# A tuned attention and feed-forward kernel: the last four key heads gathered by small DMAs, value products in pairs, another layer norm write and start-up order

## The chip, the cores and the metric

The kernel runs on one core of a Trainium2 chip. The metric is the device time of one execution in microseconds (us). The span in a profile is a little shorter (165.6 us for an execution of 167.3 us). In the profiles PE is TensorE, the matrix engine (PEld: its weight loads), DVE is VectorE, ACT is ScalarE, POOL is GpSimd and SP is SyncE, which issues most DMAs (data transfers) of this kernel from one queue, one after the other. The issue time of a DMA is how long its queue is occupied with starting it. PSUM banks hold PE's products until DVE or ACT has copied them. A run is called slow when it is over 1.5% above the fastest run of the same kernel.

## The reference, cut to what matters

```python
def _A_ref(x, wqkv, wo):                      # attention: 16 heads of 28 features
    W, dil = 8, 2                             # 8 keys back, every second one
    qkv = (x @ wqkv) ...                      # split into q, k, v
    idx = pos[:, None] - off[None, :]         # off = 0, 2, ..., 14
    logits = einsum("bhsd,bhswd->bhsw", q, kg) * scale
    attn = softmax(where(mask, logits, -1e9))
    return einsum("bhsw,bhswd->bhsd", attn, vg) ... @ wo

def _B_ref(x, w1, b1, w2, b2):                # feed forward, 448 -> 1792 -> 448
    return gelu(x @ w1 + b1) @ w2 + b2

xn = layernorm(x)                             # x: 1 x 2048 x 448
return x + _A_ref(xn, wqkv, wo) * silu(_B_ref(xn, ...))
```

## The kernel before: the parts that the argument touches

The sequence is cut into four chunks of 512 positions and, for attention, into 17 units of 121 queries. While the second FFN product of one chunk runs, the attention units of that chunk are laid between. PE's work in program order for one chunk (`n = c + 1` is the chunk whose q, k and v are being made):

```python
for c in range(3):
    feed_forward_1(c, ps, ...)          # 14 tiles of w1, gelu, the first q/k pair of the next chunk,
                                        # wo jobs of the chunk before
    qk_pair(n, 1, True, DD)
    for i in range(5):                  # five attention units
        b = next(units)
        if i == 0:
            E = qk_unit(b, lambda: qk_pair(n, 2, False, ...))   # scores S, exp and mask on ACT and DVE
            ...
            qk_pair(n, 3, True, DA)     # the fourth q/k pair stands between S and psO
        else:
            E = qk_unit(b)
            norm()
            ffn2_job(4 * c + i - 1)     # ps_y
            v_job(next(vs))             # one value product a unit
            if n + 1 < NC:
                ln_apply(4 * n + 3 + i)
                ln_dma(4 * n + 3 + i)   # DMA transpose on SP, into xnT
        norm = av_unit(b, E)            # psO
    ...
    ps = ffn1(n, 0, True)
```

Loads and stores, all issued by SP, in order:

```python
def late_loads():                       # before: issued before the first chunk's FFN
    nc.sync.dma_start(b2bc[:], ...)
    nc.sync.dma_start(x_sb[3][:, :, :], dram_rows(x_par, 12, 4))
    for g in range(4):
        for h in range(4):              # 16 loads of 28 rows from DRAM
            r = (4 * g + h) * DH
            nc.sync.dma_start(wo[32 * h + 1:32 * h + 1 + DH, g, :], A_wo[r:r + DH, :])

def wo_put(t, ps, cs=slice(0, D)):
    sg = ...
    o_t = work.tile([P, D], BF16, name="o_t", tag="o_t", bufs=3)    # three output buffers
    nc.vector.tensor_tensor(out=o_t[:, cs], in0=xt(t)[:, cs], in1=sg[:, cs], op=ALU.add)
    nc.sync.dma_start(dram_rows(out_par, t, 1)[:, 0, cs], o_t[:, cs])
```

The softmax here doesn't subtract the row's maximum and nothing guards it: scores larger than these inputs give would overflow.

Of the kernel before, what the change touches and what calls it, by code (L numbers as in the profile page):

```python
# [8 lines left out]
F32 = mybir.dt.float32  # L9
# [19 lines left out]
EPS = 1e-5  # L29
NG = 12  # L30


@with_exitstack
def kernel(
# [37 lines left out]
    g_sb = [big.tile([P, D], BF16, name=f"g_{i}") for i in range(NG)]  # L72
    wraw = work.tile([P, KT, 2 * D + 8], BF16, name="wraw", tag="stage", bufs=1)
    wv = big.tile([P, KT, D], BF16, name="wv")
    wqk = big.tile([P, KT, 2 * H, 32], BF16, name="wqk")
    w1 = big.tile([P, KT, F], BF16, name="w1")
# [19 lines left out]

    nc.vector.memset(wraw[:, :, 2 * D:2 * D + 8].bitcast(U32), 0)
    nc.vector.memset(wz[:].bitcast(U32), 0)
# [7 lines left out]
    for w in range(2):  # L106
        nc.sync.dma_start(wraw[64 * w:64 * w + 64, 3, D * w:D * w + D], A_wqkv[384:448, D * w:D * w + D])
    nc.sync.dma_start(b1r[:], B_b1.rearrange("(m f) -> m f", f=P))
    nc.sync.dma_start(x_sb[1][:, :, :], dram_rows(x_par, 4, 4))
    for c0, c1 in ((0, F // 2), (F // 2, F)):  # L110
        nc.sync.dma_start(w1[:, 0:3, c0:c1], B_w1[0:384, c0:c1].rearrange("(k p) f -> p k f", p=P))
        for r in (0, 64):
            nc.sync.dma_start(w1[r:r + 64, 3, c0:c1], B_w1[384:448, c0:c1])
    nc.sync.dma_start(x_sb[2][:, :, :], dram_rows(x_par, 8, 4))
    nc.sync.dma_start(w2[:, :, :], B_w2.rearrange("(m p) c -> p m c", p=P))

# [10 lines left out]
    nc.vector.memset(wv[64:128, 3, :].bitcast(U32), 0)  # L127
    nc.vector.memset(wraw[0:64, 3, D:D + 8].bitcast(U32), 0)
    nc.vector.memset(wo[:, :, :].bitcast(U32), 0)
# [4 lines left out]
    def late_loads():  # L134
        nc.sync.dma_start(b2bc[:], B_b2.rearrange("(o d) -> o d", o=1).to_broadcast((P, D)))
        nc.sync.dma_start(x_sb[3][:, :, :], dram_rows(x_par, 12, 4))
        for g in range(4):
            for h in range(4):
                r = (4 * g + h) * DH
                nc.sync.dma_start(wo[32 * h + 1:32 * h + 1 + DH, g, :], A_wo[r:r + DH, :])  # L140
# [27 lines left out]
    def ln_apply(t):  # L168
        nc.vector.tensor_scalar(xnb[t % 4][:, 0:D], xt(t), mv[:, t, 0:1], rstd[:, t:t + 1],
                                op0=ALU.subtract, op1=ALU.mult)  # L170

        nc.vector.tensor_copy(xnb[t % 4][:, D:512], xnb[t % 4][:, D - 64:D])

# [12 lines left out]

    def qk_weights(which, kt):

        r = slice(0, P) if kt < 3 else slice(64 * which, 64 * which + 64)
        src = wraw[r, kt, D * which:D * which + 32]  # L190
        nc.vector.tensor_copy(wqk[r, kt, H * which:H * which + H, :],
                              bass.AP(src.tensor, src.offset, [list(src.ap[0]), [DH, H], [1, 32]]))

# [18 lines left out]

    def qk_put(c, g, w, ps, copies):
        copies[w]((qT, kT)[w][:, g, LEAD + c * CH:LEAD + (c + 1) * CH], ps[w][:, :])  # L214

    def qk_pair(c, g, even, copies):

        ps = [psB.tile([P, CH], F32, name="ps_qk", tag="B") for _ in range(2)]
        for f in ((qk_full, qk_rest), (qk_rest, qk_full))[not even]:
            f(c, g, ps, f is (qk_full, qk_rest)[not even], copies)  # L220

    DA, DD = (nc.vector.tensor_copy, nc.scalar.copy), (nc.vector.tensor_copy, nc.vector.tensor_copy)

    def v_mm(b):
        ps = psB.tile([P, D], F32, name="ps_v", tag="B")
        o = LEAD + QB * b - 7
        for kt in range(KT):
            nc.tensor.matmul(ps[:, :], xnT[:, kt, o:o + P], wv[:, kt, :],  # L228
                             start=(kt == 0), stop=(kt == KT - 1))
        return ps  # L230
# [4 lines left out]
    def v_job(b):  # L235
        v_put(b, v_mm(b))


# [37 lines left out]

    def ffn2_job(t, put=True):
        tt = t % 4
        ps = psB.tile([P, D], F32, name="ps_y", tag="B")
        for m in range(MT):  # L280
            nc.tensor.matmul(ps[:, :], hT[:, m, tt * P:(tt + 1) * P], w2[:, m, :],  # L281
                             start=(m == 0), stop=(m == MT - 1))
        if put:
            ffn2_put(t, ps)
        return ps

# [104 lines left out]
    def feed_forward_1(c, ps, wos):  # L391

        nc.scalar.preload_act_table_set(SET_GELU)
        gelu(0, ps)
        for k in range(1, MT // 2):
            if (c, k) in ((0, 6), (1, 4), (2, 4)):

                qk_pair(c + 1, 0, True, DD)
            odd = k in {0: (1, 3, 5, 6), 3: (1, 3, 5)}.get(c, (1, 3, 4, 6))
            ps = ffn1(c, k, not odd)  # L400
            gelu(k, ps)
            if c + 2 < NC and k in (1, 3):
                for t in range(4 * c + 7 + k, 4 * c + 9 + k):
                    ln_stats(t)
            if k in ((3, 5, 6) if c == 3 else (4,)):
                for _ in range(4 if c == 2 else 2):
                    if wos:
                        wo_job(wos.pop(0))
            if c and k in (3, 5):
                silu_job(4 * (c - 1) + k - 3)  # L410
                silu_job(4 * (c - 1) + k - 2)
        nc.scalar.preload_act_table_set(SET_EXP)


    with tc.manual_schedule(engines={ENG.PE, ENG.Activation, ENG.DVE, ENG.Pool, ENG.SP}):
        nc.scalar.preload_act_table_set(SET_EXP)
        busy(9)
        ln_stats(0)
# [14 lines left out]
        ln_rstd(3, 1)  # L433
        v_put(0, v0)
        ln_apply(2)
        pT.append(ln_tr(2))
        v1 = v_mm(1)
        ln_put(2, pT[2])
        v_put(1, v1)
        ln_apply(3)  # L440
        pT.append(ln_tr(3))
        v2 = v_mm(2)
        ln_put(3, pT[3])
        v_put(2, v2)
        v_job(3)
        pb = psB.tile([P, MT], BF16, name="pb", tag="B")
        nc.tensor.transpose(pb[:, :], b1r[:, :], ident[0:MT, 0:MT])
        for which in range(2):
            for kt in range(KT):
                qk_weights(which, kt)  # L450
        y_sb = work.tile([P, 4, D + 4], F32, name="y", tag="stage", bufs=1)
        late_constants()
# [9 lines left out]
        for t in range(4, 8):  # L462
            ln_apply(t)
            ln_dma(t)
        late_loads()

        units = iter(range(NB))
        for c in range(3):
            feed_forward_1(c, ps, [[], [0, 1], [2, 3, 4, 5]][c])
            n = c + 1  # L470
            qk_pair(n, 1, True, DD)
            norm = lambda: None
            vs = iter(range(4 * n, 4 * n + (5 if c == 2 else 4)))
            for i in range(5):
                b = next(units)
                if i == 0:
                    tail = []
                    E = qk_unit(b, lambda: qk_pair(n, 2, False, (nc.vector.tensor_copy, lambda *a: tail.append(a))))
                    if n + 1 < NC:
                        ln_rstd(4 * n + 4, 4)  # L480
                    nc.scalar.copy(*tail[0])
                    qk_pair(n, 3, True, DA)
                else:
                    E = qk_unit(b)
                    norm()
                    ffn2_job(4 * c + i - 1)
                    v_job(next(vs))
                    if n + 1 < NC:
                        ln_apply(4 * n + 3 + i)
                        ln_dma(4 * n + 3 + i)  # L490
                norm = av_unit(b, E)
            norm()
            for b in vs:
                v_job(b)
            ps = ffn1(n, 0, True)
        feed_forward_1(3, ps, [6, 7, 8, 9, 10, 11])
# [58 lines left out]
```

## Time and profile before

| | before |
|---|---|
| median of four runs | 167.72 us (167.32 to 167.9) |
| span in the profile | 165.6 us |
| PE busy | 158.9 us, 96% of the span |
| chain that ended last | 83% PE |
| granted clock of PE | 1.000 |

### The profile page before, as it was taken

Reading aid. Unit: us, or ns where it says so; the run is one execution under the profiler, and the core shown is the slowest. Engines: PE = TensorE matmul, PEld = TensorE weight load, DVE = VectorE, ACT = ScalarE, POOL = GpSimd, SP = SyncE. Lnnn points to the kernel's source line nnn. Section 1 sums busy time; section 2 is a strip of 40 time slices with the busy share of each in tenths; the row PEclk is TensorE's granted clock in tenths of the full one; section 3 lists DMA queues with packets and bytes.
Section 4 is the critical chain, followed back from the end, with each engine's and each line's share of the span. In section 5 each row is a group of like instructions: output and inputs, shape, how many; then the busy total and the mean of one; then the engine's idle time right before and its main releaser. Section 6 shows DMA issues by size and latency. Waiting matters only on the chain.

```text
span 165.6 us, 3242 instructions
## 1 busy us (share of the span) xinstructions
PE 158.9 (96%) x1290; PEld 71.8 (43%) x1301; DVE 112.9 (68%) x256; ACT 125.9 (76%) x198; POOL 4.5 (3%) x16
## 2 busy tenths in 40 slices
PE   6899999999999999999999999999999999999990
PEld 2343333345554334445554334335555334445570
DVE  5967890497888638687888308877777507678893
ACT  3773698598887795998887795698888698698830
POOL 7002000000000000000000000000000000000000
PEclk9999999999999999999999999999999999999999
DMA  5999995520111100100211100300000002020011
GB/s 134 302 306 267 325 190 93 164 44 4 32 36 32 32 0 4 55 0 0 36 32 32 36 0 0 112 1 4 0 4 0 0 0 60 31 83 0 4 55 55
DMA packets 15963, 10.62 MB, mean 64 GB/s; under 512 B 7500, under 2 KB 15948, under 8 KB 15948
## 3 DMA queue, kind: packets, MB, share of 16 engines
q1 hardware_dynamic: 15660, 10.18, 24.0%
q10 hardware_dynamic: 288, 0.23, 0.5%
q8 instruction: 10, 0.16, 0.4%
q14 instruction: 5, 0.04, 0.1%
HBM read 7.00 MB, written 1.84 MB: 53 GB/s over the span
## 4 chain that ended last, share of the span: by engine, by line
PE 83%; ACT 7%; DVE 5%; DMA 2%; issue 1%; DVEq 0%
PE ps_y L281 23%; PE ps_h L249 21%; PE ps_qk L197 11%; PE ps_v L228 8%; PE ps_s L331 6%; PE ps_h L258 4%; PE S L355 3%; PE psO L370 3%; ACT hT L264 3%; PE ps_qk L207 3%; DMA x<-in_A_x_dram 2%; ACT th L310 1%; DVE sg L337 1%; DVE st L161 1%; ACT L509 1%
## 5 line engine op out<-in xcount | busy, mean ns | idle before, releaser
L264 ACT ACTIVATE hT<-ps_h,b1f 128x512 bf16<-128x512 f32 x56 | 34.1, 695 | 10.1 <-PE ps_h L258 7.3
L249 PE MATMUL ps_h<-xnT,w 128*128 128x512 bf16 x161 | 39.3, 380 | 0.5 <-issue 0.2
L281 PE MATMUL ps_y<-w,hT 128*128 128x448 bf16 x196 | 39.5, 353 | 0.0
L361 ACT ACTIVATE E<-S 128x976 bf16<-128x976 f32 x34 | 31.6, 983 | 2.1 <-PE S L355 0.8
L281 PEld LDWEIGHTS <-hT 128*128 128x128 bf16 x196 | 18.0, 98 | 16.7
L249 PEld LDWEIGHTS <-w 128*128 128x128 bf16 x168 | 15.0, 98 | 22.1 <-issue 6.4
L363 DVE TENSOR_TENSOR E<-E,mk_gen 128x976 bf16<-128x976 bf16 x30 | 20.0, 666 | 6.7 <-ACT E L361 6.5
L197 PE MATMUL ps_qk<-xnT,wqk 128*128 128x512 bf16 x92 | 22.2, 380 | 0.3 <-issue 0.2
L379 DVE TENSOR_TENSOR oT<-psO,den 128x484 bf16<-128x484 f32 (+1 forms) x17 | 11.3, 662 | 10.1 <-ACT den L378 10.1
L214 DVE CAST qT<-ps_qk 128x512 bf16<-128x512 f32 x16 | 11.0, 687 | 9.5 <-PE ps_qk L207 8.4
L228 PE MATMUL ps_v<-wv,xnT 128*128 128x448 bf16 x68 | 15.7, 353 | 0.1
L311 DVE SCALAR_TENSOR_TENSOR g<-th,y 128x448 bf16<-128x448 bf16 x13 | 7.6, 621 | 10.8 <-ACT th L310 10.8
L337 DVE SCALAR_TENSOR_TENSOR sg<-ps_s,g 128x448 bf16<-128x448 f32 (+2 forms) x17 | 10.1, 592 | 7.0 <-PE ps_s L331 6.9
L233 ACT CAST vw<-ps_v 128x448 bf16<-128x448 f32 x17 | 9.1, 533 | 6.9 <-PE ps_v L228 6.8
L197 PEld LDWEIGHTS <-wqk 128*128 128x128 bf16 x96 | 8.9, 98 | 11.5 <-issue 1.8
L331 PE MATMUL ps_s<-wo,oT 128*128 128x448 bf16 (+2 forms) x68 | 13.4, 342 | 0.0
L377 ACT ACTIVATE den<-den 128x484 f32<-128x484 f32 (+1 forms) x17 | 10.3, 605 | 4.0 <-DVE den L374 4.0
L374 DVE STREAM_SHUFFLE den<-psO 128x484 f32<-128x484 f32 (+1 forms) x17 | 11.7, 695 | 0.0
L378 ACT ACTIVATE den<-den 128x484 f32<-128x484 f32 (+1 forms) x17 | 10.3, 606 | 0.5
L161 DVE BATCH_NORM_STATS2 st<-x 128x6 f32<-128x448 bf16 x16 | 9.8, 610 | 0.9 <-DMA x<-in_A_x_dram 0.8
L331 PEld LDWEIGHTS <-oT 128*128 128x128 bf16 x68 | 6.4, 98 | 5.9 <-issue 0.2
L228 PEld LDWEIGHTS <-xnT 128*128 128x128 bf16 x68 | 6.3, 98 | 6.0 <-ACT xnT L181 0.6
(71 smaller groups left out, 139.8 us busy)
## 6 DMA issues: line engine op xcount, KB each, us to landing
out_dram<-o_t SPq DMA_DIRECT2D x15, 112.0 KB
w<-in_B_w_dram SPq DMA_DIRECT2D x1, 1568.0 KB
x<-in_A_x_dram SPq DMA_DIRECT2D x3, 448.0 KB
w<-in_B_w_dram SPq DMA_DIRECT2D x2, 672.0 KB
wraw<-in_A_wqkv_dram SPq DMA_DIRECT2D x1, 672.0 KB
w<-in_B_w_dram SPq DMA_DIRECT2D x4, 112.0 KB
wo<-in_A_wo_dram SPq DMA_DIRECT2D x16, 24.5 KB
wv<-in_A_wqkv_dram SPq DMA_DIRECT2D x1, 336.0 KB
```

The lines of the kernel that those rows point to most:

```text
L161: nc.vector.bn_stats(out=st[:], in_=xt(t))
L197: nc.tensor.matmul(ps[w][:, :], wqk[:, kt, 16 * w + 4 * g:16 * w + 4 * g + 4, :], xnT[:, kt, LEAD + c * CH:LEAD + (c + 1) * CH], start=(fi ...
L228: nc.tensor.matmul(ps[:, :], xnT[:, kt, o:o + P], wv[:, kt, :], start=(kt == 0), stop=(kt == KT - 1))
L249: nc.tensor.matmul(ps[i][:, :], w1[:, kt, m * P:(m + 1) * P], xnT[:, kt, LEAD + c * CH:LEAD + (c + 1) * CH], start=(first and kt == 0), st ...
L264: nc.scalar.activation(hT[:, m, :], ps[i][:, :], ACT.Gelu_apprx_tanh, bias=b1f[:, m:m + 1])
L281: nc.tensor.matmul(ps[:, :], hT[:, m, tt * P:(tt + 1) * P], w2[:, m, :], start=(m == 0), stop=(m == MT - 1))
L331: nc.tensor.matmul(ps[:, 0:n], oT[:, g, t * P:(t + 1) * P], wo[:, g, cs], start=(g == 0), stop=(g == 3))
L337: nc.vector.scalar_tensor_tensor(out=sg[:, cs], in0=ps[:, 0:cs.stop - cs.start], scalar=0.5, in1=g_sb[t % NG][:, cs], op0=ALU.mult, op1=AL ...
L361: nc.scalar.activation(ev, Sp[p2][:, :, :, 0:QW], ACT.Exp, scale=SCALE)
L363: nc.vector.tensor_tensor(out=ev, in0=ev, in1=mkb, op=ALU.mult)
L374: nc.vector.stream_shuffle(den[:, :, 0:n], psO[:, :, 0:n], [0] * 32)
L379: nc.vector.tensor_tensor(out=oT[:, :, QB * b:QB * b + n], in0=psO[:, :, 0:n], in1=den[:, :, 0:n], op=ALU.mult)
```

## The change

Its intent is to take matmul slots from PE. A head has 28 features in a slot of 32 columns. The four spare columns of 28 slots take the weights of the last four k heads, 4 features a slot, so the fourth k projection costs no matmul of its own; 28 small copies a chunk put the rows where the scores expect them. The fourth q/k pair becomes q alone. Value products are made in pairs. The wo loads move behind the first unit. The layer norm writes its last 64 features twice directly instead of copying them. In the start-up the first value results are copied later and two of them use the other PSUM pool. The core of the diff (cut):

```diff
+    def k3_rows(c, g, w):
+        j = 4 * w + g
+        cols = slice(LEAD + c * CH, LEAD + (c + 1) * CH)
+        for h in range(4):
+            nc.sync.dma_start(kT[32 * h + 4 * j:32 * h + 4 * j + 4, 3, cols],
+                              (qT, kT)[w][32 * h + DH:32 * h + 32, g, cols])
...
     def qk_put(c, g, w, ps, copies):
...
         copies[w]((qT, kT)[w][:, g, LEAD + c * CH:LEAD + (c + 1) * CH], ps[w][:, :])
+        if c:
+            k3_rows(c, g, w)
...
     def ln_apply(t):
-        nc.vector.tensor_scalar(xnb[t % 4][:, 0:D], xt(t), ...)
-        nc.vector.tensor_copy(xnb[t % 4][:, D:512], xnb[t % 4][:, D - 64:D])
+        last = x[:, D - 64:D].unsqueeze(1).to_broadcast((P, 2, 64))
+        for o, i in ((xb[:, 0:384], x[:, 0:384]), (xb[:, 384:512]..., last)):
+            nc.vector.tensor_scalar(o, i, mv[:, t, 0:1], rstd[:, t:t + 1], ...)
...
+            if c < 3 and k == (6 if c == 0 else 5):
+                q3_job(c + 1, nc.vector.tensor_copy)
...
-            qk_pair(n, 1, True, DD)
+            qk_pair(n, 1, n == 1, DD)
...
-                    qk_pair(n, 3, True, DA)
+                    late[0]()
+                    v_pair(4 * n)
+                    if c == 0:
+                        late_loads()
                 else:
...
-                    v_job(next(vs))
+                    if i == 2:
+                        v_pair(4 * n + 2)
...
-            ps = ffn1(n, 0, True)
+            ps = ffn1(n, 0, False)
```

## The prediction

> **What bounds the kernel now.** I read the page's busy shares first, then the chain that ended last, then stretches of the chain and of the timeline. The page says PE is busy 158.9 us of a span of 165.6 us, and the chain agrees:
>
> ```profile
> PE 83%; ACT 7%; DVE 5%; DMA 2%; issue 1%; DVEq 0%
> PE ps_y L281 23%; PE ps_h L249 21%; PE ps_qk L197 11%; PE ps_v L228 8%; PE ps_s L331 6%; PE ps_h L258 4%; PE S L355 3%; PE psO L370 3%; ACT hT L264 3%; PE ps_qk L207 3%; DMA x<-in_A_x_dram 2%; ACT th L310 1%; DVE sg L337 1%; DVE st L161 1%;
> ```
>
> From about 10 us to 152 us the chain is almost only TensorE, one matmul group after the other; the granted clock is 1.000. So a matmul taken away is worth its full length, as long as nothing else then becomes late. The chain in order of time gives the lengths I use, in one attention unit (scores S, FFN product ps_y, value product ps_v, attention product psO), in a q/k pair, and where four 64-row matmuls stand together:
>
> ```profile
> 12.73 0.61 PE ps_qk L207 x4
> 13.34 2.69 PE ps_qk L197 x12
> 16.03 0.54 PE ps_qk L207 x4
> ...
> 30.90 1.29 PE ps_qk L197 x6
> 32.20 0.32 PE ps_qk L207 x2
> 32.52 0.33 PE S L355 x16
> ...
> 40.69 0.33 PE S L355 x16
> 41.02 2.75 PE ps_y L281 x14
> 43.77 0.76 PE ps_v L228 x4
> 44.53 0.33 PE psO L370 x16
> ...
> 67.44 0.93 ACT th L310 x2
> 68.37 1.17 ACT hT L264 x2
> 69.53 0.04 issue
> 69.58 0.39 PE S L355 x14
> ```
>
> A full 512-column matmul is 1.29/6 = 0.215 us, a 448-column one 0.76/4 = 0.19 us. Two 64-row matmuls run side by side but cost 0.32 us alone and 0.54 us as two couples, so about 0.1 us is lost per change of tile shape. The last lines are the other kind of place: at 69.5 us S waits for ScalarE, which has to finish a gelu before the score bank is free; the timeline shows S stretched to 0.67 us there, against 0.39 us elsewhere, 0.28 us lost. It happens again at 108.2 us.
>
> How much room VectorE and ScalarE have in a unit shows in the same unit (40.62 to 44.79 us) in the timeline:
>
> ```profile
> 41.05 1.86 ACT L361 ACTIVATE E<-S 128x976 bf16<-128x976 f32 x2
> 41.44 0.18 DVE L172 COPY xnb<-xnb 128x64 bf16<-128x64 bf16 x1
> 41.54 0.70 DVE L374 STREAM_SHUFFLE den<-psO 128x484 f32<-128x484 f32 x1
> ...
> 42.95 0.67 DVE L363 TENSOR_TENSOR E<-E,mk_gen 128x976 bf16<-128x976 bf16 x1 [0.16 <-ACT E L361]
> 43.44 0.61 ACT L378 ACTIVATE den<-den 128x484 f32<-128x484 f32 x1
> 43.61 0.92 PE L228 MATMUL ps_v<-wv,xnT 128*128 128x448 bf16 x4
> 44.08 0.66 DVE L379 TENSOR_TENSOR oT<-psO,den 128x484 bf16<-128x484 f32 x1 [0.46 <-ACT den L378]
> 44.46 0.40 PE L370 MATMUL psO<-E,vw 128*32 128x122 bf16 x16
> ```
>
> The second mask ends at 43.62 us and psO, which needs it, starts at 44.46 us: slack 0.84 us. The view of stretches gives DVE 3.51 and ACT 3.50 busy in this 4.17 us. The unit is thus bound by TensorE by a small margin only.
>
> **What the Trainium skill says.** "TensorEngine Tiling (Array Packing)", Key Properties: changing the tiling mode drains TensorE. The trace agrees, with the 0.1 us above. "TensorE: Matmul & The Clock Gate", Back-to-back issue gap: N/2.4 + 2.5 ns warm, 215.8 ns for 512 columns; the trace has 0.215 us. "DMA: Bandwidth & Descriptors", Anatomy of one DMA: about 2 us fixed per DMA, mostly the write receipt, and any semaphore wait sits on the issuing sequencer, so a transfer that waits holds up those behind it. No run yet shows this for a small copy within SBUF; but the 16 small loads of wo are this kernel's nearest relative:
>
> ```profile
> L140 SPq DMA_DIRECT2D wo<-in_A_wo_dram x16: 314/383/646, 27.3 to 35.1; - x16
> ```
>
> These are minimum, median and longest issue in ns and the first and last start. 15 steps in 7.8 us, of which 1.1 us is a wait for an earlier load by the view of SP's waits: 6.7/15 = 0.45 us each.
>
> **The change part by part.** A head has 28 features in a slot of 32 columns. The four spare columns of 28 slots (16 of q, 12 of k) now hold the 4 x 28 features of the last four k heads, so for chunks 1 to 3 the fourth k projection is computed inside matmuls that run anyway. Small SBUF copies move those rows into place: 7 slot groups x 4 heads = 28 DMAs of 4 rows x 1 KB per chunk, 84 in all.
>
> (1) The fourth pair (7 matmul slots: 6 full, one couple) becomes q alone with 4 full matmuls. (2) Value products go in pairs, with their 64-row rests side by side: 6 x 0.19 + 0.30 = 1.44 us for two. Per chunk, before: pair 1.29 + 0.32 = 1.61, two v jobs 2 x 0.76 twice = 3.04, sum 4.65. After: q alone 4 x 0.215 = 0.86, two v pairs 2.88, sum 3.74. So 0.91 us per chunk, 2.7 us in three chunks. The slots alone would give 9 x 0.215 + 6 x 0.19 = 3.1 us; the difference is the additional change of tile shape in the v pairs.
>
> (3) wo jobs move behind the next FFN product, and ScalarE loses two k copies per chunk (0.57 and 0.59 us). The S waits at 69.3 and 108.2 us should go: 0.56 us. In the last chunk one change of tile shape falls away, 0.1 us.
>
> (4) Start. ScalarE now copies xnT before the v results, and v1 and v3 use the other PSUM pool. Before, the fourth xnT copy stood behind a vw copy (9.28 to 9.81 us), and PE waited from 9.3 to 10.36 us for it; that gives about 0.5 us. The q/k weights follow at 9.99 us from a DMA that lands no earlier, so I count 0.4 us. Layer norm as two independent writes instead of 448 columns plus a dependent copy: 0.52 us before per tile, by the starts of consecutive tiles (19.76, 20.28); after, an estimated 0.27 + 0.17 us. It shortens VectorE, not TensorE. The two more warm-up matmuls (0.2 to 0.43 us each) end near when the first transpose can start (5.55 us): zero. The five extra copies of spare columns are off the path.
>
> Sum of gains: 2.7 + 0.56 + 0.1 + 0.4 = 3.8 us.
>
> Against this: (5) Units 1, 3 and 4 of a chunk (of five, counted from 0) have no v job, so their TensorE time falls from 4.17 to 0.33 + 2.75 + 0.33 = 3.41 us, below the 3.5 us that VectorE is busy. The 0.84 us of slack becomes 0.08 us. The loop is shuffle 0.70, log and exponential on ScalarE 1.26, oT 0.58, y 0.53, layer norm 0.44, with semaphore gaps some 3.6 us before the next shuffle can start. Also unit 3 starts behind two v copies on ScalarE (1.1 us), and its S exponential is late by 0.3 us. Walking the engines' orders through the units with these durations I get waits of PE of 0.3 us (unit 3), 0.5 us (unit 4) and 0.3 us (the next FFN product's PSUM bank), 1.1 us in chunks 1 and 2; before has about 0.15. Chunk 3 has no layer norm, and its units wait for (6) anyhow: nothing more. So 2 x 1.1 - 0.45 = 1.75 us given back.
>
> (6) The gather. In the last chunk (c = 2, keys from 1536 on) unit 12 is the first to need the new rows, the third unit. Count from the end of the last FFN product, T0. The copies of q and k of group 1 end near T0 + 2.7 and 3.4 us, since VectorE first finishes four wo outputs and two gates. Then SP has 16 DMAs (groups 1 and 2): 16 x 0.45 = 7.2 us, so issued by T0 + 9.9, landed some 1 to 1.5 us later, T0 + 11. TensorE wants them at about T0 + 9.3 (psO of unit 10 at 5.4, one unit of 3.5, and the first scores). At 0.45 us that is a wait of 1.7 us; at the median issue of 0.38 us it is 0.6 us. I count 1.0 us. In the other two chunks the first user is unit 4 or 8, the fifth and fourth unit, and there is room. In chunk 1, wo (16 x 0.45) and the chunk 2 transposes (1.2 us each) queue behind the 28 copies: 29.5 + 28 x 0.45 = 42.1, x and wo to 50, transposes to 56, landed by 58; needed at 58.3. Just in time.
>
> (7) The first psO of a chunk waits for gelu, table load (1.28), exponentials (1.86) and mask (0.67) with one pair less work to hide it: 0.3 us in all.
>
> Given back: 1.75 + 1.0 + 0.3 = 3.05 us. Net 3.8 - 3.05 = 0.75 us: 167.68 - 0.75 = 166.9 us.
>
> **The rivals.** (a) Only TensorE matters: all 3.8 us come, 163.9 us. For it: 83% of the chain. Against it: 0.08 us of slack in the short units. (b) The SP queue is the bound: at the 0.55 us that the 64-row loads took to issue (546 ns, two loads of wraw), unit 12 waits over 3 us, and chunk 2's transposes land about 3 us late: 170 us. For it: everything is issued from one queue, in order. Against: the median small load is 0.38 us. (c) VectorE and ScalarE take the units over entirely and the gather is hidden: 165.9 us.
>
> **Range and chances.** From (a) with a bit of waiting to (b) with part of its waits: 164.5 to 169.2 us. Faster by over 2% needs under 164.4 us, nearly all of the gain: 0.13. Slower by over 2% needs 171.1 us, more than (b): 0.05. Within 2%: 0.82.
>
> **What would show it.** In the profile after: PE busy time of ps_qk and ps_v smaller by about 3 us in sum; psO of units 3 and 4 starting 0.3 to 0.6 us after ps_y ended, with DVE E or ACT E as what it waited for; PE waiting for a DMA into kT before the scores of unit 12; the issue time of the small copies, 0.38 to 0.45 us; S no longer stretched at the chunk starts; the first q/k matmul earlier by 0.4 us. If PE shows no gaps in the units and none at unit 12, rival (a) holds and I am too slow by 3 us; if copies take 0.55 us or more, or the transposes come late, I am too fast.

## More of the kernel before

The prediction reads the chain and the engines' rows. Three more readings are needed for what follows. The first is the order of SP's queue, from the timeline (start in us, length in us from the first issue of the group to the end of the last, how many).

```profile
27.30 8.16 SPq L140 DMA_DIRECT2D wo<-in_A_wo_dram  x16
41.65 13.69 SPq L184 DMA_TRANSPOSE xnT<-xnb  x4
```

SP is done with the wo loads at 35.5 us. After that it waits for each tile of the layer norm and transposes it at once; the four transposes are spread over 13.69 us because the tiles become ready one by one. SP has a lot of free time. The second reading is the granted clock in two stretches (columns: stretch, its length, busy time of PE, PEld, DVE, ACT and POOL with the number of instructions, granted clock, DMA share, GB/s).

```profile
64.60:78.20 13.60, 13.49 (x136) 5.94 (x136) 10.22 (x19) 11.29 (x18) 0.00 (x0) 1.00 0.06 18
121.20:146.50 25.30, 25.19 (x195) 11.18 (x186) 14.85 (x31) 20.97 (x34) 0.00 (x0) 1.00 0.07 20
```

PE is busy in practically all of both stretches and its clock is 1.00. The third reading is a table of landmarks of PE, which later sections use. They are starts of groups in the timeline: the first q/k pair of chunk 1 at 27.51 us, the first FFN tile of chunk 1 at 53.12, the scores of unit 5 at 69.30, the first FFN tile of chunk 2 at 90.45, the scores of unit 10 at 108.16, the first FFN tile of chunk 3 at 130.07.

## The result, and the profile after

The changed kernel is correct and took 182.87 us (median of four runs, 181.0 to 184.02) against 167.72 us for the kernel before. The ratio is 1.087 (95% interval 1.077 to 1.097): slower by 15 us. Ratios here are the mean time of one kernel's fast runs over the mean time of the other's fast runs in the same rounds, so they are not quite the ratio of the medians.

From the page of the changed kernel: the busy time of the engines, the granted clock in 40 slices of 4.55 us (9 is full speed), and the share of the chain by engine.

```profile
PE 165.0 (91%) x1280; PEld 73.2 (40%) x1291; DVE 115.6 (64%) x261; ACT 122.5 (67%) x192; POOL 4.5 (2%) x16
PEclk9999999999999957999999999987969999999999
PE 53%; DVE 19%; ACT 13%; DMA 7%; issue 3%; SPq 3%; DVEq 0%
```

PE has 10 instructions fewer than before and yet is busy 6.1 us longer: something slows its instructions. The clock row names it. The chain runs through PE for 53% where it was 83%.

The landmarks say where the time goes. Each row is the difference of two starts in the timeline; the last column is a run described below, the changed kernel without its copies.

| stage of PE | before | after | no copies |
|---|---|---|---|
| start to the q/k pair of chunk 1 | 27.51 | 27.90 | 27.32 |
| to the first FFN tile of chunk 1 | 25.61 | 25.53 | 25.53 |
| FFN of chunk 1, to the scores of unit 5 | 16.18 | 24.68 | 17.57 |
| units 5 to 9, to the first FFN tile of chunk 2 | 21.15 | 19.75 | 19.74 |
| FFN of chunk 2, to the scores of unit 10 | 17.71 | 19.09 | 19.08 |
| units 10 to 14, to the first FFN tile of chunk 3 | 21.91 | 29.46 | 20.01 |
| the rest | 35.5 | 35.6 | 35.9 |

The whole loss sits in two stages: the FFN of chunk 1 (8.5 us longer than before, 7.1 longer than without copies) and the last five units (7.6 and 9.5 us).

The queue of SP answers for both. In the timeline of the changed kernel:

```profile
30.43 2.62 SPq L210 DMA_DIRECT2D kT<-qT  x4
...
45.86 2.44 SPq L210 DMA_DIRECT2D kT<-kT  x4
...
48.84 9.02 SPq L143 DMA_DIRECT2D wo<-in_A_wo_dram  x16
57.95 5.16 SPq L188 DMA_TRANSPOSE xnT<-xnb  x4
```

One such copy is issued in 0.577 us (minimum, median and maximum in ns, first and last start):

```profile
L210 SPq DMA_DIRECT2D kT<-qT x48: 577/577/707, 30.4 to 128.2; - x48
```

The 28 copies of chunk 1 occupy SP from 30.43 to 48.30 us: 17.87 us, or 0.64 us each with the steps between them. Behind them come one load of x, 16 loads of wo, and only then the four transposes of chunk 2, from 57.95 us where before they began at 41.65. They land when PE has long been waiting. These are the waits of PE, from its timeline (the bracket is how long PE stood idle before the group, and what released it):

```profile
64.65 0.61 PE L226 MATMUL ps_qk<-xnT,wqk 64*128 64x512 bf16 x2 [4.05 <-DMA xnT<-xnb]
...
121.24 1.82 PE L275 MATMUL ps_v<-wv,xnT 128*128 128x448 bf16 x6 [2.18 <-DVE qT L236]
...
130.65 0.22 PE L398 MATMUL S<-qT,kT 28*128 28x122 bf16 x1 [2.25 <-DMA kT<-kT]
...
132.58 0.26 PE L398 MATMUL S<-qT,kT 28*128 28x122 bf16 x1 [0.47 <-DMA kT<-kT]
```

The first is the late transpose. The last two are the late copies of unit 12; between them stand two more of 0.38 and 0.42 us. The second names DVE, and DVE in its turn waits for SP:

```profile
117.28 2.60 SPq L384 DMA_DIRECT2D out_dram<-o_t  x4
119.13 0.39 DVE L383 TENSOR_TENSOR o_t<-x,sg 128x448 bf16<-128x448 bf16 x1 [4.07 <-DMA out_dram<-o_t]
```

Four output tiles are to be stored in that stretch and there are three buffers. The first store sits on SP behind 12 copies, so it is issued at 117.28 us, and DVE stands for 4.07 us in front of the fourth output. The q and k results that it should copy next stay in PSUM, and the value products have no free bank.

The waits of PE sum to 4.05 + 2.18 + 2.25 + 0.38 + 0.42 + 0.47 = 9.75 us. That is not 15. The rest is in the clock. The same two stretches as before:

```profile
64.60:78.20 13.60, 13.50 (x59) 4.84 (x64) 5.72 (x10) 5.04 (x9) 0.00 (x0) 0.77 0.05 15
121.20:146.50 25.30, 21.74 (x221) 10.20 (x221) 15.18 (x29) 14.09 (x21) 0.00 (x0) 0.87 0.02 4
```

Cut into half microseconds, the clock is 1.00 or 0.50, apart from the pieces in which it changes: it is 0.50 from about 63.9 to 70.7 us, from 121.9 to 125.3 and from 132.2 to 135.6. PE loses (1 - 0.77) x 13.6 = 3.1 us in the first stretch and (1 - 0.87) x 25.3 = 3.3 us in the second. Waits and clock together make 16.2 us; the span of the profiled run grew by 182.0 - 165.6 = 16.4 us. This only adds up PE's time; it does not say that each part, taken away, would be gained in full (the run with dummy matmuls below shows that it would not). The clock also goes with the spread of the changed kernel's runs over 1.7%: its four runs have mean clocks of 0.978, 0.969, 0.962 and 0.961 at 181.0, 182.04, 183.69 and 184.02 us (the last was called slow and is not in the ratio).

"TensorE: Matmul & The Clock Gate", Part 1: The HAM clock gate, says that the array falls to half speed after an idle window of about 3.4 us, that the window is free-running, and that its activity monitor knows no speeds between. The trace agrees: 0.50 and 1.00 only, and the low stretches are about 6.8, 3.4 and 3.4 us long, so one or two such windows. The waits before the last two are shorter than a window, though; the last section returns to this.

### The profile page after: what moved, and what is told of

It reads as the page before. It is cut to its first block, busy times and chain, and to the rows that moved or that the text cites. A ratio compares the mean times of both kernels' runs of the same rounds, so it can differ in the third digit from the quotient of the medians.

```text
span 182.0 us, 3352 instructions
## 1 busy us (share of the span) xinstructions
PE 165.0 (91%) x1280; PEld 73.2 (40%) x1291; DVE 115.6 (64%) x261; ACT 122.5 (67%) x192; POOL 4.5 (2%) x16
## 4 chain that ended last, share of the span: by engine, by line
PE 53%; DVE 19%; ACT 13%; DMA 7%; issue 3%; SPq 3%; DVEq 0%
PE ps_y L326 16%; PE ps_h L294 9%; PE ps_qk L216 7%; PE ps_v L275 4%; DVE st L164 4%; PE ps_s L374 3%; DMA xnT<-xnb 3%; PE S L398 3%; ACT den L421 3%; ACT hT L309 3%; DVE xnb L176 3%; ACT den L420 2%; PE psO L413 2%; SPq L210 2%; PE ps_v L259 2%
## 5 line engine op out<-in xcount | busy, mean ns | idle before, releaser
L326 PE MATMUL ps_y<-w,hT 128*128 128x448 bf16 x196 | 41.2, 364 | 0.0
L294 PE MATMUL ps_h<-xnT,w 128*128 128x512 bf16 x161 | 40.1, 389 | 0.8 <-issue 0.6
L406 DVE TENSOR_TENSOR E<-E,mk_gen 128x976 bf16<-128x976 bf16 x30 | 19.4, 664 | 10.0 <-ACT E L404 10.0
L294 PEld LDWEIGHTS <-w 128*128 128x128 bf16 x168 | 15.6, 99 | 23.1 <-issue 7.5
L216 PE MATMUL ps_qk<-xnT,wqk 128*128 128x512 bf16 x74 | 19.4, 400 | 1.0 <-issue 0.5
L264 ACT CAST vw<-ps_v 128x448 bf16<-128x448 f32 x17 | 8.4, 539 | 10.8 <-PE ps_v L279 10.1
L216 PEld LDWEIGHTS <-wqk 128*128 128x128 bf16 x78 | 7.0, 100 | 11.3 <-issue 5.2
L398 PE MATMUL S<-qT,kT 28*128 28x122 bf16 x272 | 8.3, 220 | 3.5 <-DMA kT<-kT 3.5
L303 PE MATMUL ps_h<-xnT,w 64*128 64x512 bf16 x56 | 10.4, 387 | 0.3 <-DVE oT L422 0.2
L275 PE MATMUL ps_v<-wv,xnT 128*128 128x448 bf16 x36 | 8.3, 368 | 2.2 <-DVE qT L236 2.2
```

Source lines behind the costliest of these rows:

```text
L216: nc.tensor.matmul(ps[w][:, :], wqk[:, kt, 16 * w + 4 * g:16 * w + 4 * g + 4, :], xnT[:, kt, LEAD + c * CH:LEAD + (c + 1) * CH], start=(fi ...
L275: nc.tensor.matmul(ps[i][:, :], xnT[:, kt, o:o + P], wv[:, kt, :], start=(kt == 0), stop=False)
L294: nc.tensor.matmul(ps[i][:, :], w1[:, kt, m * P:(m + 1) * P], xnT[:, kt, LEAD + c * CH:LEAD + (c + 1) * CH], start=(first and kt == 0), st ...
L326: nc.tensor.matmul(ps[:, :], hT[:, m, tt * P:(tt + 1) * P], w2[:, m, :], start=(m == 0), stop=(m == MT - 1))
L398: nc.tensor.matmul(Sp[h // 2][:, h % 2, g, 0:QW], kT[r, g, o - 7:o - 7 + P], qT[r, g, o:o + QW], start=True, stop=True)
L406: nc.vector.tensor_tensor(out=ev, in0=ev, in1=mkb, op=ALU.mult)
```

## The experiments

The theory after reading the two traces: (A) the copies are issued one after the other on SP, at 0.64 us each, and delay what stands behind them in the same queue (transposes, stores, the last copies themselves); PE then waits, and after a wait it runs at half clock. A rival (B): the rest of the change, the pairing and the order, costs the time. A rival (C): the copies are slow by their movement, or their traffic disturbs others, whoever issues them. All runs below gave correct outputs by the comparison; two are wrong in the last k heads of chunks 1 to 3, and the comparison still passed them, so it is not sensitive to those four heads.

### The copies left out

```diff
-        if c:
-            k3_rows(c, g, w)
+    nc.gpsimd.memset(kT[:, 3, LEAD + CH:LEAD + S].bitcast(U32), 0)     # once, at the start
```

> Wrong result on purpose: the 84 small copies are left out, and the fourth k group of chunks 1 to 3 is zeroed once by GpSimd. Everything else is the changed kernel. Theory A (the small copies occupy the SP queue, 0.635 us each from start to start, and hold up transposes, stores and the scores): the 15 us come back and the time is 164.5 to 167 us, clock 1.00, no wait of PE for xnT or kT over 0.5 us. Rival B (paired value products, short units, the new order or the layer norm cost the time): still above 175 us.

Measured: 166.88 us (166.77 to 167.68; before 167.14), ratio 0.9991 (0.9956 to 1.0026), clock 1.00. All of the 15 us hangs on the copies, and B falls. But the gain against before that the prediction expected without its step (6), 1.75 us, is not there either. Two lines from PE's timeline of this run show part of it, at the end of unit 4 and the start of the next FFN:

```profile
52.52 0.39 PE L412 MATMUL psO<-E,vw 128*32 128x122 bf16 x14 [0.27 <-DVE E L405]
...
53.38 0.39 PE L302 MATMUL ps_h<-xnT,w 64*128 64x512 bf16 x1 [0.15 <-DVE oT L421]
```

PE waits for the mask of a short unit and then for the bank of the last attention product. The table above has the balance: five units save 1.41 us (unit 5 to 9) and 1.90 us (unit 10 to 14), and the FFN stage ahead of them grows by 1.39 and 1.37 us, because q alone stands there now (0.86 us) and its first tile takes 0.85 us from its first matmul (52.85) to the next group (53.70), where such a pair elsewhere takes 0.32.

### The copies on GpSimd

```diff
-            nc.sync.dma_start(kT[32 * h + 4 * j:..., 3, cols],
+            nc.gpsimd.dma_start(kT[32 * h + 4 * j:..., 3, cols],
```

> Same copies, same bytes, but issued from GpSimd, which is idle after 14 us; correct result. Theory A: the transposes and the stores are on time again, so the wait of 4 us for xnT and the wait of 4 us for the output buffer go; what remains depends on how fast GpSimd issues: 166 to 168 us if 28 copies take under 15 us, up to 174 us if a copy takes about 1 us, with a wait for kT before the scores of unit 12. Rival C (moving the 84 small blocks itself, its engines or its landing, costs the time): 178 us or more.

Measured: 170.85 us (169.23 to 171.51), ratio 1.020 (1.014 to 1.026), clock 0.99. Twelve of the fifteen microseconds are gone although the same bytes move between the same places. From the line of the copies in this run's trace (issue time in ns: minimum, median, maximum; first and last start) and from PE's timeline at unit 12:

```profile
L210 POOL DMA_DIRECT2D kT<-qT x48: 518/518/650, 30.2 to 115.4; - x48
```

```profile
117.58 0.22 PE L398 MATMUL S<-qT,kT 28*128 28x122 bf16 x1 [0.49 <-DMA kT<-kT]
```

The waits for transposes and for output buffers are gone, since those have SP to themselves; unit 12 still waits for its last rows, as 28 x 0.52 us is still long. A copy lands 1.7 us after its issue in the median. That is A; C falls as the main cause. Part of what is left is again the clock. The four waits at unit 12 sum to only 1.34 us (0.49, 0.31, 0.27 and 0.27), and behind them the clock is 0.50 from about 119.2 to 122.6 us, so that the 14 FFN matmuls there take 4.48 us in place of 2.82. Together this is 3.0 of the 3.9 us by which the span (169.0) exceeds that of the run without copies (165.1). The fastest of the four runs, 169.23 us, had a mean clock of 1.00.

### Only the wo loads on GpSimd

```diff
-                nc.sync.dma_start(wo[32 * h + 1:32 * h + 1 + DH, g, :], A_wo[r:r + DH, :])
+                nc.gpsimd.dma_start(wo[32 * h + 1:32 * h + 1 + DH, g, :], A_wo[r:r + DH, :])
```

> Only the 16 loads of wo move from SP to GpSimd; correct result. Theory A: in chunk 1 the four transposes leave SP about 9 us earlier, so PE's wait of 4.05 us for xnT goes and with it the half-clock stretch behind it (clock 0.77 from 64.6 to 78.2 us, about 3 us): 174.5 to 177 us; the waits in the last chunk (output buffer 4.1 us, kT 2.3 us) stay. Rivals B and C: no change, 181 us or more.

Measured: 183.77 us (179.78 to 185.32), and three of the four runs were slow. It was a badly built experiment. The wait at chunk 2 did vanish, but the loads have nothing to wait for, and GpSimd issued them from 12.7 us on, into the start-up loads. From PE's timeline (of a slow run):

```profile
30.69 1.54 PE L216 MATMUL ps_qk<-xnT,wqk 128*128 128x512 bf16 x6 [3.47 <-DMA xnT<-xnb]
```

The transposes of chunk 1 were late instead, and a new wait of 3.47 us with a stretch of lowered clock took the place of the old one.

### The wo loads on GpSimd, held back

```diff
+        nc.gpsimd.tensor_copy(gate[:, 0:56], qT[:, 2, LEAD + CH:LEAD + CH + 56])   # waits for q of chunk 1
+        nc.gpsimd.memset(wo[:, :, 0:2].bitcast(U32), 0)
...
-                nc.sync.dma_start(wo[32 * h + 1:...], A_wo[r:r + DH, :])
+                nc.gpsimd.dma_start(wo[32 * h + 1:...], A_wo[r:r + DH, :])
```

> The changed kernel with the 16 wo loads issued by GpSimd, held back by a small copy that needs q of chunk 1, so that they don't go out in the start-up as in the earlier try. Theory A (the SP queue, issue by issue, delays the chunk-2 transposes): the transposes are issued some 8 us earlier, the wait of about 4 us for xnT at the start of chunk 2's q/k goes, and with it the stretch of lowered clock after it; the last chunk's waits (2.2 and 2.3 us, lowered clock) stay: 174 to 178 us. Rival C (the copies are slow because of their movement, not their issue): the wait stays and the time is at 181 us or above.

Measured: 180.08 us (178.85 to 181.21), ratio 1.076 (1.072 to 1.080). In the trace the transposes start at 48.26 us in place of 57.95, the wait of 4.05 us is gone, the clock stays at 1.00 up to 124 us, and the scores of unit 5 start at 70.37 us, 7.7 us earlier than in the changed kernel. The mechanism is as expected, the size is not: 2.8 us by the medians. Of the 7.7 us, 1.4 came back by the first FFN tile of chunk 2, as chunk 2 now outruns its own copies at unit 8 (four waits of 0.26 to 0.41 us that were not there), and unit 12 is done 6.1 us earlier. After it the clock is now at 0.50 for two windows, from 124.7 to 131.5 us, and these fall on work: the profiled spans differ by 5.1 us (176.9 and 182.0; each kernel's profiled run is at another end of its spread than the other's). A wait that is removed leaves those behind it, and they may turn worse.

### Eight output buffers in addition

```diff
-        o_t = work.tile([P, D], BF16, name="o_t", tag="o_t", bufs=3)
+        o_t = work.tile([P, D], BF16, name="o_t", tag="o_t", bufs=8)
```

> The changed kernel with wo on GpSimd, held back (180.1 us), and 8 output buffers in place of 3. The wait of VectorE for an output buffer (4.0 us) and, behind it, PE's wait of 2.14 us before the value products of the last chunk go. Theory (SP's order of issue): the copies of the last chunk still have to be issued one after the other, 28 x 0.635 + 4 stores, from about 103.5 us: the last lands at about 125.5 to 126 us where it was at 127; so unit 12 waits longer and only 0.5 to 1.5 us come: 178.3 to 179.8 us. Rival (the short ring of output buffers was the cause of the last chunk's loss): all of the 2.1 us and part of the clock come, under 177.5 us.

Measured: 176.28 us (175.67 to 176.73), ratio 1.053 (1.051 to 1.056). 3.8 us were gained, more than A had allowed, and the rival's number is right. The wait of 2.18 us before the value products and DVE's wait for a buffer are gone, and unit 12 waits longer, as A said:

```profile
122.60 0.28 PE L401 MATMUL S<-qT,kT 28*128 28x122 bf16 x1 [3.94 <-DMA kT<-kT]
```

Its scores end 1.9 us earlier than in the run before (124.55 us in place of 126.46 for the start of the last one), not 1 to 1.5, and the span is 2.7 us shorter (174.2 in place of 176.9). The chain copies, store, buffer, DVE, q copy, next copy closed a loop on SP that I had counted only as waiting time of PE. The 1.1 us between the medians and the spans comes from the choice of run: the profiled run with the wo loads held back was its fastest (178.85 us, median 180.08), the one here was near its median (176.18). Some 9 us to the run without copies (166.88) remain, so the short ring of buffers is a part of the last chunk's loss and not all of it.

### Dummy matmuls in the waits

44 products of zeros, which nothing reads: 18 before the late transposes, 10 before the q/k products of group 2 in the last chunk, 16 before the scores of unit 12.

```diff
             if c + 1 < NC and k == (6 if c == 0 else 4):
+                if c == 1:
+                    busy(18)
...
+        if (c, g) == (3, 2):
+            for _ in range(10):
+                nc.tensor.matmul(ps[0][:, :], wz[:, 0:P], wz[:, :], start=True, stop=True)
...
+                    if c == 2 and i == 2:
+                        busy(16)
                     E = qk_unit(b)
```

> The changed kernel, correct, with 44 matmuls more that do nothing useful: 18 just before the wait for the chunk-2 transposes (18 x 0.216 = 3.9 us for a wait of 4.05), 10 before the q/k products of group 2 in the last chunk (2.2 us for the wait of 2.18 in front of the value products), 16 before the scores of unit 12 (3.5 us for waits that end 4.5 us later). Theory: the waits themselves cost about 9.5 us, and the rest of the 15 us is that TensorE runs at a lowered clock after them (13.6 us at 0.77 and 25.3 us at 0.87, 3.1 + 3.3 = 6.4 us). Matmuls in the waits keep the clock up, so more work makes the kernel faster: 175.5 to 178.5 us, and the clock is 0.99 or 1.00 in both stretches. Rival: the clock is lowered by something else that the copies bring (then it stays near 0.96 on the mean and the time is 183 us or above), or the dummy matmuls push the work behind them back by their own length (187 us).

Measured: 180.16 us (179.89 to 180.31), ratio 1.076 (1.074 to 1.078): 2.7 us faster than the changed kernel with 9.5 us more of matmuls, and the runs agree within 0.3% again. The two stretches:

```profile
64.60:78.20 13.60, 13.60 (x82) 5.50 (x81) 8.14 (x14) 8.25 (x13) 0.00 (x0) 1.00 0.07 23
121.20:146.50 25.30, 24.41 (x244) 11.41 (x244) 14.34 (x28) 16.33 (x24) 0.00 (x0) 1.00 0.01 4
```

The clock is 1.00 in both, with all copies still there. So the copies alone do not lower the clock; PE's idling does. The gain is smaller than the 6.4 us worked out from the clock. The first FFN tile of chunk 2 is 3.4 us earlier (94.49 in place of 97.86 us) and that of chunk 3 3.8 us (142.61 in place of 146.41), so only 0.4 us were gained in between. I read this as follows: the low stretch from 121.9 to 125.3 us was worth nothing, since behind it PE waits for the copies of unit 12 anyway, and the last scores of unit 12 even start 1.0 us later, counted from the first FFN tile of chunk 2 (35.7 us in place of 34.7). Slow work ahead of a wait costs as little as idle time.

### Issue time by shape

27 copies that nothing reads, in a stretch of the kernel before in which SP has nothing to do: three each of 4, 8, 16, 32, 64 and 128 rows of 1 KB within SBUF, then three each of 4, 28 and 128 rows of 896 B from DRAM.

```diff
+    for rows, src in ((4, 0), (8, 0), (16, 0), (32, 0), (64, 0), (128, 0), (4, 1), (28, 1), (128, 1)):
+        for _ in range(3):
+            if src == 0:
+                nc.sync.dma_start(scr[0:rows, k % 6, :], kT[0:rows, k % 3, LEAD:LEAD + CH])
+            else:
+                nc.sync.dma_start(scr[0:rows, k % 6, 0:D], dram_rows(x_par, 0, 1)[0:rows, 0, :])
+            k += 1
```

> The kernel before with 27 copies that nothing reads, three each of nine shapes, on SP in an idle stretch of the last chunk, to measure the issue time by shape. What the prediction used: 0.38 us median, 0.45 us by pitch, from loads of 28 rows x 896 B from DRAM. Theory: the issue time depends on where source and destination lie or on rows, not on bytes alone: SBUF to SBUF, 4 rows of 1 KB, 0.577 us as in the changed kernel, the DRAM loads of 28 rows 0.38 us. Rival: it depends on the queue's load; in an idle stretch the 4-row copies take 0.38 us as well. The time of the kernel stays at that of before plus 0 to 1 us, since nothing waits for the copies.

Measured: 167.39 us against 167.46, ratio 1.0003 (0.998 to 1.002). Issue times, minimum, median and maximum in ns:

```profile
L489 SPq DMA_DIRECT2D scr<-kT x18: 532/595/1488, 106.5 to 119.1; - x18
```

```profile
L491 SPq DMA_DIRECT2D scr<-in_A_x_dram x9: 293/384/1596, 119.8 to 124.3; - x9
```

By shape: within SBUF 0.58 to 0.72 us for 4 rows, 0.63 to 0.64 for 8, 0.53 to 0.58 for 16, 0.59 to 0.60 for 64 and for 128 rows; from DRAM 0.29 to 0.49 us for 4 rows, 0.31 to 0.38 for 28 and 0.38 to 0.43 for 128 (one of 32 rows and one of 28 took 1.5 and 1.6 us and are left out). Within SBUF the rows and the bytes hardly count: a copy of 128 KB is issued in the time of one of 4 KB. The queue in idle time is no faster than in the changed kernel, so the rival falls. That these loads from DRAM are issued faster is not a rule for every load, and the place of the source alone does not decide: the kernel's stores go from SBUF to DRAM and are issued in 0.33 us (median of the 17 in the changed kernel, maximum 0.40), while its loads of 64 rows of wraw and w1 from DRAM take 0.47 to 0.60 us. The two groups of this run also differ in the length of a row (1 KB and 896 B). Which property sets the issue time stays open; for copies with both ends in SBUF the number itself is measured.

### The copies split over two queues

```diff
-            nc.sync.dma_start(kT[32 * h + 4 * j:..., 3, cols],
+            (nc.sync, nc.gpsimd)[h % 2].dma_start(kT[32 * h + 4 * j:..., 3, cols],
```

> The changed kernel, correct, with the copies of heads 0 and 2 of each group on SP and those of 1 and 3 on GpSimd: 14 copies per chunk on each. From the measured pitch: 14 x 0.635 = 8.9 us on SP and 14 x 0.518 = 7.3 us on GpSimd in place of 17.8 and 14.5. Theory A (issue time in order on one queue): all waits for xnT, for output buffers and for kT at unit 12 vanish or stay under 0.3 us, and the time is that of the run without copies, 166.7 to 168.0 us. Rival C (movement, or interference of the copies with other traffic[...]): it stays above 168.5 us, near the run with all copies on GpSimd (170.9).

Measured: 167.69 us (167.28 to 168.26), ratio 1.0021 (1.0003 to 1.0039), clock 1.00. The same 84 copies, and 15 us are gone: issue time in order is the cause. By the ratios it is 0.2% above before and 0.3% above the run without copies. One more cost shows at the three units that first read the copied rows, here unit 4:

```profile
49.46 1.06 PE L398 MATMUL S<-qT,kT 28*128 28x122 bf16 x16
```

These scores take 0.40 us elsewhere, and 0.88 and 0.91 us at units 8 and 12. No wait for data is listed there; the trace has eight semaphore instructions of 51 ns on PE's queue of weight loads within these 16 matmuls (none in the kernel before), 0.41 us of the 0.66. That the copies of two queues make the scores wait on many semaphores is my reading; no run separates it.

### The fourth q/k products as a pair again, no copies

```diff
-                q3_job(c + 1, nc.vector.tensor_copy)
+                qk_pair(c + 1, 3, True, DA)
...
-        if c:
-            k3_rows(c, g, w)
```

> The gather is undone: no spare columns, the fourth q/k pair is computed as a pair where the changed kernel computes q alone; paired value products, order and layer norm stay; correct result. Theory A: near the kernel before, 166 to 168.5 us (against it 7 instead of 4 matmul slots per chunk, 3 x 0.75 us, compared with the run without the copies). Rival B: above 175 us.

Measured: 169.53 us (169.33 to 169.67), ratio 1.0133 (1.011 to 1.016). Against the run without copies it is 2.65 us slower by the medians (2.4 by the ratios): that is what q alone saves over a pair in three chunks, 0.8 to 0.9 us each, of which step (1) of the prediction counted 1.61 - 0.86 = 0.75. So the saving that the change was after is real. But without it the rest of the change (value pairs, shorter units, other order) loses 2.4 us against the kernel before, and the saving only fills that hole. The pair here stands in the FFN and no longer in the first unit.

### Value products one by one, no copies

The run without copies, with one value product in each of units 1 to 4 as in the kernel before (wrong in the last k heads).

```diff
-                    v_pair(4 * n)
...
-                    if i == 2:
-                        v_pair(4 * n + 2)
+                    v_job(4 * n + i - 1)
```

> The run without copies, but with one value product per unit as in the kernel before (wrong on purpose: the last k rows of chunks 1 to 3 are zero). Theory: of the gain that the prediction expected without its step (6), 1.75 us, only 0.3 us came, because units without a value product between S and psO make PE wait for E. Then with the value products back in every unit the q-alone saving shows: 165.0 to 165.9 us, ratio to before 0.987 to 0.993. Rival: the pairing is not to blame (it saves four short matmuls a chunk and costs nothing); then this run is at 166.9 or above, up to 167.6.

Measured: 169.17 us (168.69 to 169.18), ratio 1.010 (1.009 to 1.012). The theory falls: without the pairs it is about 2 us slower than the run without copies, not faster (2.3 us by the medians, 1.9 by the ratios; the two ran in different rounds). The waits in the short units are gone, but the first unit of a chunk now has nothing between its scores and psO but one q/k pair, and waits twice, by 0.71 and 0.63 us:

```profile
74.19 0.39 PE L412 MATMUL psO<-E,vw 128*32 128x122 bf16 x14 [0.63 <-DVE E L405]
```

The fourth q/k pair, which the change takes from this place, was not only work; it covered the exponential and the mask. The first value pair takes over that role.

### Another bank for the first FFN tile

```diff
     def ffn1_tiles(k):
-        if k in (0, 3):
+        if k in (1, 3):          # these use the common banks, the others the score banks
```

> The gather split over SP and GpSimd (167.7 us), with the first FFN tile of each chunk in the score banks and the second in the common ones, in place of first and fourth in the common ones. In the run without copies the first pair of 64-row matmuls of such a tile took 0.85 us from start to the next matmul where such a pair takes 0.31 elsewhere, because its second bank is still held by the last attention product. Theory: 0.3 to 0.5 us in each of three chunks: 166.3 to 167.2 us. Rival: the score bank is free later than that because of the last exponential, or the third gelu waits: 167.6 us or above.

Measured, on top of the split copies: 167.69 us (167.09 to 168.51), ratio 1.002 (0.999 to 1.005): a miss. In the trace the first tile's pair no longer waits, and the gain is lost 7 us later, where the q/k pair waits for a bank that a gelu still holds:

```profile
61.24 0.37 PE L226 MATMUL ps_qk<-xnT,wqk 64*128 64x512 bf16 x1 [0.20 <-ACT hT L309]
```

### Layer norm and start-up alone

The kernel before with the new layer norm writes and the new order and banks of the first value copies, nothing else.

```diff
+    def v_mm(b, pool=psB): ...
-        v_put(0, v0)                 # before ln_apply(2)
-        v1 = v_mm(1)
+        v1 = v_mm(1, psA)
         ln_put(2, pT[2])
-        v_put(1, v1)
+        v_put(0, v0)
...
+        v_put(1, v1)
+        v3 = v_mm(3, psA)
```

> The kernel before with two parts of the change alone: the layer norm that writes the last features twice, and the start-up order of the value copies. In the run without copies the first q/k products began 0.29 us earlier than in the kernel before. If these two parts carry that gain to the end, this run comes out at 166.6 to 167.0 us where before is at 167.2 (ratio 0.997 to 0.999). Rival: the early start is eaten by the first units, and the ratio is 0.999 to 1.001. Either way it is inside 2%.

Measured: 166.93 us (166.78 to 167.42) against 167.34 us (167.08 to 167.5), ratio 0.9981 (0.9967 to 0.9995). Small, but it is the fastest kernel of this study that computes everything, and it beats both.

## Why the prediction was wrong

The prediction said 166.9 us, in a range of 164.5 to 169.2; the changed kernel took 182.87 us.

**The step that failed is (6), the gather.** It took "16 x 0.45 = 7.2 us" from the issue of the wo loads. Those come from DRAM. The copies go from SBUF to SBUF, and these were issued every 0.64 us; the run of shapes has 0.53 to 0.72 us for copies within SBUF at any size against 0.29 to 0.49 us for its loads from DRAM (each without one outlier). The prediction named the doubt itself (no run had yet shown a small copy within SBUF) and then chose the nearest relative by size, which was issued faster. Its own sign of being wrong came true twice: copies of 0.55 us or more, and late transposes. The landing that it counted, 1 to 1.5 us after the issue, was right: the last copy is issued by 131.3 us and the last wait for it ends at 132.58. The figure of 2 us that it cites stands on that page for DMAs issued from GpSimd; 1.7 us is what they took here.

From there three consequences were missed, in this order of cost.

- "In chunk 1, wo (16 x 0.45) and the chunk 2 transposes queue behind the 28 copies ... Just in time": at 0.64 us, 28 copies take 5.3 us more than at 0.45, and the wo loads took 9.0 us in place of 7.2. So the copies ended at 48.3 us (counted: 42.1), the loads at 57.9 (50), the transpose that PE needed was there at 64.65 (58), and PE, ready at 60.6 (58.3), waited 4.05 us. A plan that ends "just in time" has no margin against the one number that had not been measured, and it should have been the largest risk in the range. Holding the wo loads off that queue removed this wait.
- The stores in the last chunk were not in the account at all. They share SP with the copies, and with three output buffers a late store stops DVE, which stops the q copies and the value products (2.18 us). Eight buffers removed that wait and more.
- Unit 12 waited 3.5 us in sum instead of the 1.0 us of step (6).

**The granted clock was not in any step.** The view of before had it at 1.000, and the prediction took it as constant. It isn't when PE waits: by the clock, 6.4 us of PE's time in the loss is half-speed work after the waits. The run with dummy matmuls brought the clock back to 1.00. It made the kernel faster by 2.7 us, not by 6.4, since it adds work and since one slow stretch lay ahead of another wait.

**Rival (b)** named the right cause, SP's queue as the bound with everything issued in order from it, and the reason that spoke for it. Its size, 170 us, was too small by 13 us: it took 0.55 us an issue (near the truth, though also taken from loads from DRAM), left out the stores, and left out the clock. The chance of 0.05 for slower by over 2% was too low for a rival with a known cause.

**The rest, without the gather**, can be held against the run without copies. By the prediction's terms it should have gained 3.8 - 1.75 - 0.3 = 1.75 us. The spans differ by 0.5 us (165.1 and 165.6).

- Steps (1), (2), (3), (5) and (7) make 2.73 + 0.56 - 1.75 - 0.3 = 1.24 us in the three chunks; the table has 0.08, 0.02 and 1.90 - 1.37 = 0.53, together 0.63 us. (1) was right by the run with the pair again. (5) was right in kind: psO stretches in the short units from 0.40 to 0.57 us or waits 0.27 us. (3) came too: the scores of units 5 and 10 take 0.40 us in the run without copies where they took 0.67. The largest error among them is the first FFN tile, which now begins with its 64-row pair and waits for a bank: (5) had 0.3 us for it in two chunks, and each FFN stage shows 0.5 (0.85 against 0.32). Of the missing 0.6 us, that is 0.4.
- (7): 0.3 us was expected, and nothing is seen; psO of unit 5 takes 0.59 us without copies, 0.61 before. The value pair covers it. Without one there it is 1.34 us.
- (4): 0.4 us predicted for the start; 0.19 us by the landmark, and 0.4 us by the medians of the run with only these parts.
- The 0.1 us for the last chunk became a loss of 0.3 us (the last row of the table); there too the first FFN tile starts with the 64-row pair, and it takes 0.66 us to the next group.

## What to carry to other kernels

Count the issue time of every DMA on its queue as work of an engine, with a duration measured on a transfer of the same kind (both ends and shape), and then list what else stands in that queue behind it: loads, transposes, stores and through them the ring of output buffers. A chain that is "just in time" on such a queue is the place to spread over two queues before anything else; here this alone took back 15 us. When PE is the bound, a wait can cost twice, once as a wait and once as slow work after it, unless another wait follows. How long it must be these traces do not settle: waits of 1.34 us in sum (the copies on GpSimd) were followed by 3.4 us at half clock, and one of 2.14 us (the wo loads held back) was not.

## What the Trainium skill lacked or had wrong

- "DMA: Bandwidth & Descriptors", Issuing engines are not separate DMA queues: it says that using several engines saves only the time on the sequencer, "which is usually small relative to the DMA itself". For small copies within SBUF it is a third of it, and it adds up: an issue of 0.577 us on SP (every 0.64 us) or 0.518 us on GpSimd, a median of 1.7 us to landing when issued from GpSimd, and 28 of them in a row; splitting them over two engines took the kernel from 182.87 to 167.69 us.
- The same page, Anatomy of one DMA (which describes the GpSimd path): it gives about 50 ns for dispatch and calls descriptor generation small and variable. The runs show an issue of 518 ns on GpSimd (and 505 to 512 ns for most of the 16 wo loads from DRAM). No page that I read splits SP's issue time by the ends of the copy (this one has a single cycle count per copy, in its part on trn3): 0.53 to 0.72 us within SBUF for 4 to 128 rows of 1 KB, 0.29 to 0.49 us for rows of 896 B from DRAM, 0.33 us for stores of such rows to DRAM.
- "TensorE: Matmul & The Clock Gate", Part 1: confirmed by the clock of 0.50 or 1.00 and low stretches of 3.4 and 6.8 us. What it lacks is how much idling within a window is enough. It names an idle window of about 3.4 us; here waits of 2.18 us (up to 121.24 us), of 2.25 us followed by three of about 0.4, and, in the run with the copies on GpSimd, of 1.34 us in four pieces were each followed by a low stretch, while 2.14 us in the run with the wo loads held back was not.
- No page that I read has the cost of several semaphore waits inside a group of short matmuls: with eight semaphore instructions of 51 ns among them, 16 score matmuls took 1.06 us in place of 0.40 (that the one causes the other is not shown).
